# Copying the spread 1/sum out of PSUM on ScalarE, and multiplying on GpSimd

## The chip, the cores and the metric

The kernel runs on one core of a Trainium2 chip. A core has five engines that work side by side: TensorE (PE, matrix products into PSUM), VectorE (DVE), ScalarE (ACT), GpSimd (POOL, which works on SBUF alone here) and SyncE (SP, which issues the transfers in this kernel). Each takes its instructions in the order in which they are written. The metric is the device time of one execution in microseconds. Times of before are the median of three executions; all durations below come from one further execution that was profiled.

## What is computed

Attention with rotary positions over 2 batches of 8 heads, 576 positions and 64 features a head; its output is turned into 1152 tokens of 512 features and goes through two feed-forward layers.

```python
q_rot, k_rot = (rotate(q), rotate(k))
scores = scale * np.matmul(q_rot, k_rot.transpose(0, 1, 3, 2))
scores = scores - np.max(scores, axis=-1, keepdims=True)
attn = np.exp(scores)
attn = attn / (np.sum(attn, axis=-1, keepdims=True) + 1e-09)
x = np.matmul(attn, v)            # then (B, S, H * D) -> 1152 x 512
h = np.maximum(x @ w_in, 0.0)
x = h * h @ w_out                 # 512 -> 2048 -> 512
out = (x @ w_a) * (x @ w_b) @ w2_out   # 512 -> 1536 -> 512
```

## The kernel before

**Stages.** The sixteen heads are worked in eight pairs, p = 0 to 7. A pair's 576 query rows of two heads are 1152 rows, in nine tiles of 128: chunks c = 0 to 3 have one tile of each head, chunk 4, the tail, has 64 rows of each head in one tile. After the attention come the feed-forward layers, from about 136 us on (units of the first product are mixed in with the end of the attention) to the end, all on TensorE in products that are each split into three (high and low parts of both factors).

**A chunk.** TensorE writes scores of a chunk into PSUM tiles `s` (two slots of two banks each, so one chunk fills both). VectorE finds the row's minimum of the negated scores while it moves them to SBUF (L427), which frees the slot; ScalarE takes the exponential in place and sums it (L432, into `st`); VectorE transposes the result in blocks of 32 (L448, into `PT_wb` or `PT_acc`). In the same loop step TensorE multiplies V with the transposed exponentials of the pair before (`times_v`, L480, into four banks `av`).

**The sums.** The division comes after the product with V. `recip` inverts the 1152 sums of a pair on VectorE (L509, L510) and cuts them into three bf16 pieces on GpSimd (`part`, L513 to L516). `flip` turns the pieces on TensorE (L525) into a PSUM tile `r`, and ScalarE copies them to SBUF (`rows`, L309). `spread` has nine small products of TensorE (L539) write 1/sum over all partitions of that same tile `r`, which takes one of the two score slots at the tail of each pair from 2 on: at the tail of pair p it flips pair p - 1 and spreads pair p - 2. VectorE multiplies the attention's output `xf` with it straight out of PSUM (L546, two instructions of 128x288), and with that the slot is free. Then `x` is made: ScalarE rounds `xf` to the high part (L572), GpSimd subtracts (L569) for the low part. Pairs 6 and 7 are spread after the last scores, into the free columns 192 to 480 of two `av` banks; the flip of pair 7 uses a corner of `AV[2]`.

**Loads.** SyncE's queue carries everything that comes from HBM: `X` (queries, keys and their swapped halves, four loads of 288 KB a pair, into two buffers `g0` and `g1`), `V` (four loads of 288 KB a pair, each behind a tiny copy of ScalarE, L458, that says that the place is free) and the raw weights (512 KB each, three buffers). GpSimd multiplies and adds `X` into the rotated queries and keys (`rotate`, L358 and L359).

**What sets the order.** The program builds a list of operations with costs, dependencies and buffers (`Plan`), and a greedy planner assigns engines and an order from them; the instructions of TensorE, ScalarE, VectorE and GpSimd are kept in that order. SyncE is not in that list: its transfers were put in order by the framework's own scheduler.

Of the kernel before, what the change touches and what calls it, by code (L numbers as in the profile page):

```python
# [7 lines left out]
F32 = mybir.dt.float32  # L8
# [8 lines left out]
P = 128  # L17
# [22 lines left out]
VAT = ((0,), (1,), (2, 3), (), ())  # L40
WARM = (16, 2, 5, 3)
# [203 lines left out]
def attention_moe_moe2_kernel(ctx: ExitStack, tc: tile.TileContext, qk, rope, vq, ident_in, sel_in, w_in, w_out, w_a, w_b, w2_out, out):  # L245
# [39 lines left out]
    def narrow():  # L285
# [10 lines left out]
        "raw": 3, "bits": 2, "sums": 1, "cl": 2, "wa": NWA, **{f"P{k}": 1 for k in range(NPR)}, "v": NV, "u": 2,  # L296
# [157 lines left out]
    def load_part(p, c):  # L454
        ex, st = EXP[p, c][1], ST[p]
        for a in VAT[c]:
            r = slice(32 * a, 32 * a + 32)
            w = pl.op("ACT", ("us", 0.2), lambda e, r=r: e.copy(V4[r, p % 2, 0, 0, 0:1], st()[r, 1, 2 * c + 1:2 * c + 2]), ex[-1:] + ([AVD[p - 2]] if p > 1 else []))  # L458
            w.soon, w.anchor = 1.8, SDONE[p, c]
            LV.setdefault(p, []).append(dma(288, lambda e, r=r: e.dma_start(out=V4[r, p % 2], in_=vq[p]), [w]))  # L460
        if c < 4 and p + 2 < NPAIR:
            if c == 0:
                load_qk_done[p + 2] = load_qk(p + 2)
            before = EXP[order[5 * p + c - 1]][1] if p + c else []
            load_qk_done[p + 2][PLANES[c]] = LX[p + 2, c](before)
# [65 lines left out]
    def spread(p, slots, at):  # L531
# [11 lines left out]
        ends = []  # L543
        for r in range(2):
            q = slice(r * 288, r * 288 + 288)
            m = pl.op("DVE", ("p", 288), lambda e, r=r, q=q: e.tensor_tensor(out=xf()[:, q].rearrange("p (b n) -> p b n", b=2), in0=at[r](), in1=xf()[:, q].rearrange("p (b n) -> p b n", b=2), op=ALU.mult), [o] + XOK[p])  # L546
            m.soon, m.anchor = 0.9, o
# [3 lines left out]
            ends.append(m)  # L551
# [400 lines left out]
    def last_spread(p, slots=None):  # L952
        pair = [lambda r=r: AV[r]()[:, 192:480].rearrange("p (b n) -> p b n", b=2) for r in range(2)]
        b = [Buf("av", None)] if slots is None else slots
        ends = spread(p, b, pair)
        if slots is None:
            pl.op(None, None, None, ends, rel=b)
# [14 lines left out]
    for n, (fn, *a) in enumerate(steps):  # L972
# [6 lines left out]
        if n == FILL[1]:  # L979
            flip(p, [], lambda: AV[2]().bitcast(BF16)[0:27, 896:1024])  # L980
# [25 lines left out]
    with tc.manual_schedule(engines={getattr(mybir.EngineType, e) for e in ("PE", "Activation", "DVE", "Pool")}):  # L1006
        pl.run({"PE": pe, "ACT": act, "DVE": dve, "POOL": pool, "SP": nc.sync})
# [65 lines left out]
```

## Time and profile before

| What | us |
|---|---|
| median of three runs (561.53 to 564.47) | 563.22 |
| the profiled execution | 563.06 |
| its span (first to last instruction) | 561.0 |
| TensorE busy in the span | 541.4 |
| VectorE busy | 433.1 |
| ScalarE busy | 277.7 |
| GpSimd busy | 302.4 |

The span is what the rows below are counted in; 2.1 us of the execution lie around it. A busy TensorE is not TensorE at its best: matrix products overlap, and the clock that it is granted differs. What matters is therefore read by stretch: in which one TensorE waits, and for whom. The page of the profile gives shares for the whole span; the views of the trace give single instructions with their start, their duration and, in brackets, how long the engine was idle before them and who released it.

### The profile page before, as it was taken

To read this page: it belongs to the slowest core of one execution; us is meant where nothing else is said; L and a number is where in the kernel's file an instruction comes from. 1 tells how busy PE (TensorE), PEld (TensorE's weight loads), DVE (VectorE), ACT (ScalarE), POOL (GpSimd) and SP (SyncE) were. 2 spreads that over 40 slices of the span, in tenths; PEclk is the share of its full clock that TensorE was granted. 3 is DMA by queue.
4 is the path that set the end of the run, shared out by engine and by line. 5 is a ranking of instruction groups with operands and counts; after the bars stand their busy time and mean duration, and the time that the engine had idled before them with its cause. 6 is when DMAs were issued, how large, how long until landed. Compare 5 with 4: busy or idle time off the path is not lost.

```text
span 561.0 us, 13032 instructions
## 1 busy us (share of the span) xinstructions
PE 541.4 (96%) x5318; PEld 486.5 (87%) x5318; DVE 433.1 (77%) x785; ACT 277.7 (49%) x652; POOL 302.4 (54%) x249
## 2 busy tenths in 40 slices
PE   7898998999999999999999999999999999999997
PEld 6565665657899999999999999999999999999986
DVE  5998798998189589858865679987897888886454
ACT  2556675777367567416612445466544454434210
POOL 3956679722187347506622465785776666565000
PEclk9999898999899999999999999999999999999999
DMA  7677865333033444413420110124341222400004
GB/s 242 190 211 212 208 197 132 102 93 99 4 114 124 139 157 143 139 52 115 147 76 20 57 39 1 60 76 131 112 140 58 103 77 76 142 10 1 1 0 168
DMA packets 18911, 58.45 MB, mean 104 GB/s; under 512 B 2313, under 2 KB 4489, under 8 KB 17828
## 3 DMA queue, kind: packets, MB, share of 16 engines
q1 hardware_dynamic: 18852, 57.63, 32.9%
q8 instruction: 41, 0.67, 0.5%
q14 instruction: 18, 0.15, 0.1%
HBM read 55.26 MB, written 2.36 MB: 103 GB/s over the span
## 4 chain that ended last, share of the span: by engine, by line
PE 82%; DVE 12%; ACT 2%; issue 2%; DMA 1%; SPq 0%; POOL 0%; DVEq 0%; POOLq 0%
PE m L674 12%; PE m L676 12%; PE m L675 12%; PE av L480 7%; PE av L674 6%; PE av L676 6%; PE av L675 6%; PE s L407 6%; PE m L883 3%; PE m L882 3%; PE m L881 3%; DVE y L569 2%; DVE PT_acc L448 2%; DVE PV L427 2%; PE av L883 1%
## 5 line engine op out<-in xcount | busy, mean ns | idle before, releaser
L569 POOL TENSOR_TENSOR g<-v,g 128x384 fp32r<-128x384 f32 (+1 forms) x39 | 47.5, 1219 | 48.7 <-ACT g L572 48.4
L432 ACT ACTIVATE PV<-PV,st 128x576 f32<-128x576 f32 x48 | 36.9, 770 | 39.0 <-DVE PV L427 37.1
L572 ACT CAST g<-v 128x384 fp32r<-128x384 f32 (+1 forms) x72 | 40.8, 568 | 30.4 <-DVE v L852 16.2
L675 PE MATMUL m<-y,w_p 128*128 128x288 f32 x152 | 44.8, 295 | 0.0
L674 PE MATMUL m<-y,w_p 128*128 128x288 f32 x152 | 44.7, 294 | 0.0
L676 PE MATMUL m<-y,w_p 128*128 128x288 f32 x152 | 44.7, 294 | 0.0
L427 DVE TENSOR_SCALAR_CACHE_REDUCE PV<-s 128x576 f32<-128x576 f32 x48 | 34.3, 750 | 6.5 <-PE s L407 6.2
L358 POOL TENSOR_TENSOR X<-X,cs_rot 128x1152 f32<-128x1152 f32 x14 | 36.8, 2635 | 0.1
L407 PE MATMUL s<-cs_rot 64*128 64x288 f32 x128 | 27.1, 435 | 6.0 <-DVE PV L427 2.8
L480 PE MATMUL av<-PT_acc,PV 32*64 32x128 f32 (+1 forms) x1152 | 28.3, 312 | 4.2 <-issue 3.0
L480 PEld LDWEIGHTS av<-PT_acc,PV 32*64 32x64 f32 x1152 | 22.2, 139 | 10.1 <-issue 7.2
L713 DVE TENSOR_TENSOR v<-m,v 128x384 f32<-128x384 f32 x32 | 17.7, 552 | 16.5 <-ACT v L712 16.5
L407 PE MATMUL s<-rot 64*128 64x288 f32 x128 | 27.5, 461 | 2.8 <-DVE PV L427 1.5
L722 DVE TENSOR_TENSOR oacc<-m,oacc 128x512 f32<-128x512 f32 (+1 forms) x32 | 21.6, 679 | 10.8 <-PE m L883 10.7
L675 PEld LDWEIGHTS m<-y,w_p 128*128 128x128 f32 x152 | 28.5, 188 | 1.0
L676 PE MATMUL m<-g,w_o 128*128 128x384 f32 (+1 forms) x92 | 29.3, 319 | 0.0
L675 PE MATMUL m<-g,w_o 128*128 128x384 f32 (+1 forms) x92 | 29.3, 318 | 0.0
L674 PE MATMUL m<-g,w_o 128*128 128x384 f32 (+1 forms) x92 | 29.3, 318 | 0.0
L674 PEld LDWEIGHTS m<-y,w_p 128*128 128x128 f32 x152 | 28.5, 188 | 0.9
L569 POOL TENSOR_TENSOR w_i<-bits_i,w_i 128x512 fp32r<-128x512 f32 x10 | 13.1, 1306 | 29.1 <-ACT w_i L572 29.0
L569 DVE TENSOR_TENSOR g<-v,g 128x384 fp32r<-128x384 f32 (+1 forms) x33 | 24.2, 732 | 5.8 <-ACT g L572 5.6
L676 PEld LDWEIGHTS m<-y,w_p 128*128 128x128 f32 x152 | 28.6, 188 | 0.0
(246 smaller groups left out, 1919.3 us busy)
## 6 DMA issues: line engine op xcount, KB each, us to landing
PV<-in_vq SPq DMA_DIRECT2D x32, 288.0 KB, 4.2
raw_i<-in_w_in SPq DMA_DIRECT2D x16, 512.0 KB, 3.7
raw_o<-in_w_out SPq DMA_DIRECT2D x16, 512.0 KB, 3.6
X<-in_qk SPq DMA_DIRECT2D x26, 288.0 KB, 4.2
raw_a<-in_w_a SPq DMA_DIRECT2D x12, 512.0 KB, 3.7
raw_b<-in_w_b SPq DMA_DIRECT2D x12, 512.0 KB, 3.6
raw<-in_w_out SPq DMA_DIRECT2D x12, 512.0 KB, 3.7
out<-oacc SPq DMA_DIRECT2D x8, 256.0 KB, 2.0
```

Of the source, the lines that this page charges most:

```text
L358: m = pl.op(where, ("s", 2 * S), lambda e, qi=qi: e.tensor_tensor(out=x()[:, :, qi, :], in0=x()[:, :, qi, :], in1=cs, op=ALU.mult), [done[ ...
L407: pe.matmul(s[h]()[:, bk, 0:288], q0, k0[h][:, bk * 288:bk * 288 + 288], start=True, stop=True)
L427: m = pl.op("DVE", ("us", 0.7), lambda e, h=h, j=j: e.tensor_scalar(out=PP[pr.k][:, h, :].rearrange("p (b n) -> p b n", b=2), in0=s[h]()[: ...
L432: x = pl.op("ACT", ("us", 0.8), lambda e, h=h, j=j: e.activation(PP[pr.k][:, h, :], PP[pr.k][:, h, :], AF.Exp, bias=st()[:, 0, j:j + 1], s ...
L480: pe.matmul(AV[a]()[half(h), q], v[r, h, b], pt[r, k:k + 4 + both, 32 * b:32 * b + 32], start=(b == 0), stop=(b == KB - 1), skip_group_che ...
L569: e.tensor_tensor(out=out_, in0=a, in1=b, op=ALU.subtract)
L572: h = pl.op("ACT", ("s", n), lambda e: e.copy(hi_(), val()), after)
L674: pe.matmul(dst, wh, mh, start=first, stop=False, skip_group_check=open_)
L675: pe.matmul(dst, wh, ml, start=False, stop=False, skip_group_check=open_)
L676: pe.matmul(dst, wl, mh, start=False, stop=last, skip_group_check=open_)
L722: return pl.op("DVE", ("p", width), lambda e: e.tensor_tensor(out=acc(), in0=dst(), in1=acc(), op=ALU.add), [o] + b.prior, rel=[b])
L883: pe.matmul(b(), gt[:, 1, c], w[:, 0, d], start=False, stop=(k == H - 1))
```

## The change

ScalarE copies the spread 1/sum out of PSUM into an SBUF tile `inv` (one buffer, two copies of 128x288 a pair). The multiplication with `xf` reads `inv` and goes to GpSimd for pairs 0 to 5, and to GpSimd or VectorE, as the planner finds, for pairs 6 and 7. SyncE joins the engines that keep the planner's order. The four loads of `X` for pair p + 2 are given places in that order: chunk 0, chunk 1 and, two of them, chunk 3 of pair p, behind the chunk's tiny copy or exponential; a lateness of 1.5 us is reckoned for loads of `X` and `V`. The last spreads go to columns 0 to 288 of their banks, and the flip of pair 7 gets a bank of its own.

```diff
+XAT = ((0,), (1,), (), (2, 3), ())
+FAR = 1.5
...
-        "raw": 3, "bits": 2, "sums": 1, "cl": 2, "wa": NWA, **{f"P{k}": 1 for k in range(NPR)}, "v": NV, "u": 2,
+        "raw": 3, "bits": 2, "sums": 1, "cl": 2, "wa": NWA, **{f"P{k}": 1 for k in range(NPR)}, "v": NV, "u": 2, "inv": 1,
...
         ex, st = EXP[p, c][1], ST[p]
+        more = p + 2 < NPAIR
+        if c == 0 and more:
+            load_qk_done[p + 2] = load_qk(p + 2)
+        w = ex[-1]
         for a in VAT[c]:
...
-            LV.setdefault(p, []).append(dma(288, lambda e, r=r: e.dma_start(out=V4[r, p % 2], in_=vq[p]), [w]))
-        if c < 4 and p + 2 < NPAIR:
-            if c == 0:
-                load_qk_done[p + 2] = load_qk(p + 2)
-            before = EXP[order[5 * p + c - 1]][1] if p + c else []
-            load_qk_done[p + 2][PLANES[c]] = LX[p + 2, c](before)
+            d = dma(288, lambda e, r=r: e.dma_start(out=V4[r, p % 2], in_=vq[p]), [w])
+            d.late = FAR
+            LV.setdefault(p, []).append(d)
+        for k in XAT[c] if more else ():
+            d = load_qk_done[p + 2][PLANES[k]] = LX[p + 2, k]([w])
+            d.late = FAR
...
-        ends = []
+        inv = Buf("inv", lambda: sb.tile([P, S], F32, tag="inv", name=f"inv{p}"))
+        ends = [pl.op("ACT", ("p", 288), lambda e, r=r: e.copy(inv()[:, r * 288:r * 288 + 288].rearrange("p (b n) -> p b n", b=2), at[r]()), [o], acq=[] if r else [inv]) for r in range(2)]
+        turned = []
         for r in range(2):
             q = slice(r * 288, r * 288 + 288)
-            m = pl.op("DVE", ("p", 288), lambda e, r=r, q=q: e.tensor_tensor(out=xf()[:, q].rearrange("p (b n) -> p b n", b=2), in0=at[r](), in1=xf()[:, q].rearrange("p (b n) -> p b n", b=2), op=ALU.mult), [o] + XOK[p])
-            m.soon, m.anchor = 0.9, o
+            ends[r].soon, ends[r].anchor = 0.9, o
+            m = pl.op("POOL" if p < NPAIR - 2 else FLEX, ("s", 288), lambda e, q=q: e.tensor_tensor(out=xf()[:, q], in0=inv()[:, q], in1=xf()[:, q], op=ALU.mult), [ends[r]] + XOK[p])
+            turned.append(m)
...
-            ends.append(m)
+        pl.op(None, None, None, turned, rel=[inv])
...
-        pair = [lambda r=r: AV[r]()[:, 192:480].rearrange("p (b n) -> p b n", b=2) for r in range(2)]
+        pair = [lambda r=r: AV[r]()[:, 0:288].rearrange("p (b n) -> p b n", b=2) for r in range(2)]
...
-            flip(p, [], lambda: AV[2]().bitcast(BF16)[0:27, 896:1024])
+            b = bank("flip", 64)
+            pl.op(None, None, None, [flip(p, [b], lambda: b().bitcast(BF16)[0:27])], rel=[b])
...
-    with tc.manual_schedule(engines={getattr(mybir.EngineType, e) for e in ("PE", "Activation", "DVE", "Pool")}):
+    with tc.manual_schedule(engines={getattr(mybir.EngineType, e) for e in ("PE", "Activation", "DVE", "Pool", "SP")}):
```

SyncE's queue in pairs 2 and 3, before (X4 is the pair 4 of queries and keys, in_vq is V, in_w_in raw weights):

```order
L332 DMA X4_431<-in_qk 128x576 x4
L332 DMA X5_676<-in_qk 128x576 x4
L583 DMA raw_i0_475<-in_w_in 128x512
L460 DMA PV_73<-in_vq 32x2304 x4
L332 DMA X6_936<-in_qk 128x576 x4
L460 DMA PV_73<-in_vq 32x2304
```

The same place after:

```order
L592 DMA raw_i0_477<-in_w_in 128x512
L466 DMA PV_73<-in_vq 32x2304
L334 DMA X4_525<-in_qk 128x576
L466 DMA PV_73<-in_vq 32x2304
L334 DMA X4_525<-in_qk 128x576
L466 DMA PV_73<-in_vq 32x2304 x2
L334 DMA X4_525<-in_qk 128x576 x2
L592 DMA raw_i1_728<-in_w_in 128x512
L466 DMA PV_73<-in_vq 32x2304
L334 DMA X5_781<-in_qk 128x576
```

The four loads of a pair's X no longer stand together; they stand between the loads of V, and those of X5 to X7 stand about one pair later.

VectorE at the tail of pair 5, before (s5_4 holds the tail's scores, s6_0 the next pair's first; r5 the spread):

```order
L427 TENSOR_SCALAR rot_69,st5_1244<-s5_4_0_1422 128x576
L448 STREAM_TRANSPOSE PT_acc_72<-small_70 128x576
L546 TENSOR_TENSOR xf3_1253<-r5_1430,xf3_1253 128x288 x2
L448 STREAM_TRANSPOSE PT_acc_72<-small_70 128x576
L448 STREAM_TRANSPOSE PT_acc_72<-rot_69 128x576
L427 TENSOR_SCALAR PV_73,st6_1508<-s6_0_1_1478 128x576
```

And after:

```order
L429 TENSOR_SCALAR rot_69,st5_1245<-s5_4_0_1427 128x576
L450 STREAM_TRANSPOSE PT_acc_72<-small_70 128x576 x2
L450 STREAM_TRANSPOSE PT_acc_72<-rot_69 128x576
L429 TENSOR_SCALAR PV_73,st6_1513<-s6_0_1_1484 128x576
L429 TENSOR_SCALAR PV_73,st6_1513<-s6_0_0_1482 128x576
```

The two multiplies are gone from VectorE. ScalarE at the same tail, before:

```order
L432 ACTIVATE small_70,st5_1244<-small_70,st5_1244 128x576 x2
L309 COPY rows4_1443<-r5_1430 27x128
L432 ACTIVATE rot_69,st5_1244<-rot_69,st5_1244 128x576
L572 CAST x_67<-xf3_1253 128x288 x2
L432 ACTIVATE PV_73,st6_1508<-PV_73,st6_1508 128x576
```

And after:

```order
L434 ACTIVATE small_70,st5_1245<-small_70,st5_1245 128x576 x2
L311 COPY rows4_1447<-r5_1435 27x128
L550 COPY inv3_1475<-r5_1435 128x288 x2
L434 ACTIVATE rot_69,st5_1245<-rot_69,st5_1245 128x576
L434 ACTIVATE PV_73,st6_1513<-PV_73,st6_1513 128x576
```

The two copies stand between the copy of the row and the tail's exponential; the rounding of `x` (L581 after) has moved to later places. TensorE's order in the attention is unchanged.

## Rows read from the trace of the kernel before

**Rows 1.** Busy us (x instructions) by stretch: PE, PEld, DVE, ACT, POOL, clock, DMA, GB/s.
```profile
40.00:145.00 105.00, 94.43 (x2212) 65.92 (x2195) 88.54 (x203) 69.75 (x220) 64.48 (x69) 0.95 0.53 145
145.00:561.00 416.00, 411.73 (x2696) 395.92 (x2695) 313.35 (x519) 190.44 (x386) 213.62 (x159) 1.00 0.25 84
```
**Rows 2.** TensorE's waits from 40 to 145 us: total us, times, longest.
```profile
PE av L480 <- issue: 4.1, 3, 2.3
PE s L407 <- DVE PV L427: 2.5, 4, 0.7
PE s L407 <- DVE bits_i L591: 2.4, 4, 0.6
```
**Rows 3.** The attention's end in order of time: start, duration, instruction, [idle before].
```profile
138.72 0.49 ACT L712 ACTIVATE v<-m 128x384 f32<-128x384 f32 x1 [1.09 <-POOL rest L514]
...
139.72 0.81 DVE L546 TENSOR_TENSOR xf<-av,xf 128x288 f32<-128x288 f32 x2
...
140.22 4.63 PE L480 MATMUL av<-PT_acc,PV 32*64 32x160 f32 x128 [1.20 <-DVE xf L546]
```
**Rows 4.** The tail of pair 5 in order of time, same columns.
```profile
103.13 0.26 ACT L309 COPY rows<-r 27x128 bf16<-27x128 bf16 x1 [0.65 <-PE r L539]
...
103.36 0.78 ACT L432 ACTIVATE rot<-rot,st 128x576 f32<-128x576 f32 x1
103.94 0.79 DVE L546 TENSOR_TENSOR xf<-r,xf 128x288 f32<-128x288 f32 x2
...
104.05 2.03 PE L407 MATMUL s<-cs_rot 64*128 64x288 f32 x8
...
105.33 0.73 DVE L448 STREAM_TRANSPOSE PT_acc<-rot 128x576 f32<-128x576 f32 x1
...
106.11 0.76 DVE L427 TENSOR_SCALAR_CACHE_REDUCE PV<-s 128x576 f32<-128x576 f32 x1
...
106.97 0.78 ACT L432 ACTIVATE PV<-PV,st 128x576 f32<-128x576 f32 x1 [1.78 <-POOL rot L359]
```
**Rows 5.** TensorE alone in order of time, 53 to 100 us.
```profile
54.61 0.49 PE L480 MATMUL av<-PT_acc,PV 32*64 32x160 f32 x5 [2.31 <-issue]
55.03 1.32 PE L407 MATMUL s<-rot 64*128 64x288 f32 x8
...
58.12 1.89 PE L407 MATMUL s<-rot 64*128 64x288 f32 x8
...
87.80 1.24 PE L407 MATMUL s<-rot 64*128 64x288 f32 x8
```
**Rows 6.** ScalarE's groups by shape: busy us, mean ns of one, idle before.
```profile
L827 ACT COPY v<-m 128x288 f32<-128x288 f32 x16 | 6.4, 400 | 41.6 <-PE m L676 41.6
```
**Rows 7.** GpSimd's groups by shape, same columns.
```profile
L358 POOL TENSOR_TENSOR X<-X,cs_rot 128x1152 f32<-128x1152 f32 x14 | 36.8, 2635 | 0.1
L569 POOL TENSOR_TENSOR x<-xf,x 128x288 fp32r<-128x288 f32 x14 | 11.0, 797 | 10.3 <-ACT x L572 10.3
```
**Rows 8.** GpSimd's fullest pair, columns as in rows 1.
```profile
84.10:101.40 17.30, 15.36 (x341) 10.36 (x342) 14.84 (x34) 11.37 (x36) 13.43 (x13) 0.90 0.45 116
```
**Rows 9.** SyncE's issues ahead of TensorE's first stop, in order of time.
```profile
42.96 1.75 SPq L332 DMA_DIRECT2D X<-in_qk  x4
...
45.30 3.70 SPq L460 DMA_DIRECT2D PV<-in_vq  x4
```
**Rows 10.** From stop to stop of TensorE, columns as in rows 1.
```profile
54.60:67.59 12.99, 11.92 (x254) 8.35 (x253) 10.07 (x25) 8.69 (x28) 7.69 (x10) 0.87 0.77 204
67.59:86.79 19.20, 17.13 (x380) 11.37 (x381) 16.34 (x39) 12.61 (x40) 15.33 (x14) 1.00 0.69 191
```
**Rows 11.** The page's DMA queue for instructions: packets, MB, share of 16 engines.
```profile
q8 instruction: 41, 0.67, 0.5%
```
**Rows 12.** After the first stop, columns as in rows 1.
```profile
56.00:59.50 3.50, 3.50 (x58) 2.50 (x56) 2.54 (x8) 2.13 (x12) 1.97 (x6) 0.51 0.40 117
```
**Rows 13.** The granted clock in 40 slices of the span, in tenths, from the page.
```profile
PEclk9999898999899999999999999999999999999999
```

## The prediction

> **What bounds the kernel now.** I read the busy time by stretch first, then TensorE's waits, then the instructions in order of time at the places where those waits lie. A pair is two heads; chunks c = 0 to 4 are its score tiles, chunk 4 its tail. From 145 us to the end TensorE is busy for 411.73 of 416 us [rows 1]: an engine that is full there gives nothing back to helpers, and time can be won there only by arriving earlier. From 40 to 145 us it is busy for 94.43 of 105 us, at a mean granted clock of 0.95. So what the change can win lies in those 105 us: 10.6 us of idleness and what the slow clock costs. The waits that the trace names are few [rows 2]: 4.1 us in three waits that nothing in the profile releases ("issue"), 2.5 us on VectorE's L427 and 2.4 us on its L591. A further 1.20 us stands at 140.22 us behind the multiply L546 [rows 3]. Before 40 us VectorE and ScalarE alternate with no multiply among them, and I leave that stretch alone.
>
> **The tail of a pair, the change's first place.** The tail of pair 5 is the pattern for pairs 3, 5 and 6 (at pair 4 a stop of TensorE lies in its place, below). The tile r5 holds the spread 1/sum and takes one of the two score slots. VectorE frees it with two L546, from 103.94 to 104.73 us [rows 4]; until then the second half of pair 6's first scores can't start, so those eight records last 2.03 us, against 1.32 us where nothing is in the way [rows 5]: a wait of 0.7 us. VectorE then transposes the tail (to 106.06) and reduces the new scores at 106.11.
> Now ScalarE copies r5 out. Its copy of the row of 1/sum ends at 103.39; two copies of 128x288 out of PSUM at 400 ns [rows 6] end at 104.19, so the slot is free 0.54 us earlier. But they stand ahead of the tail's exponential, which starts at 104.2 instead of 103.36 and ends at 104.97; with 0.1 us for the hand-over, the transpose that needs it runs from about 105.1 to 105.8 (0.73 us). VectorE, rid of 0.79 us of multiplies, waits for it, and reduces at 105.8 instead of 106.11. So of 0.79 us taken off VectorE and 0.54 us off the slot, 0.3 us is left per tail: the exponential is what is late next. Three tails: 0.9 us. The bounds are 2.1 us (the whole 0.7 us three times) and a loss of 0.6 us (each of the four instructions in that row 0.12 us longer than taken).
>
> **GpSimd's new work.** It gets two multiplies a pair of the shape of its L569, 797 ns each [rows 7], so 1.6 us. Its fullest pair, 84.1 to 101.4 us, has 13.43 us of work in 17.3 us [rows 8]; 15.0 us still fits. I cost it at nothing, the cover being 2.3 us a pair. If it runs out, ScalarE pays: the rounding of x (L581) now waits in ScalarE's queue for GpSimd, with exponentials behind it, and ScalarE's copy into the single buffer inv waits for the multiplies of the pair before.
>
> **The end of attention.** TensorE is idle until 140.22, since the last pair's output needs the banks that hold the spread for pair 6, and VectorE reads them from 139.72 on, behind its product L713, which waits for ScalarE's ReLU (138.72 to 139.21) [rows 3]. ScalarE's copies come right behind that ReLU: 139.61 and 140.01 in place of 140.1 and 140.53. That is 0.5 us; bounds 0 and 1.2 us. The flip in its own bank and the spread at columns 0 to 288 keep TensorE's order, and the eight copies that must precede that spread are done a unit earlier: nothing, and at most 0.2 us.
>
> **SyncE's queue.** This is the larger term, and the less certain. Before, the four loads of X5 go out together at 42.96 us, then w_in, then four loads of V from 45.30 [rows 9]: 8 x 288 + 512 = 2816 KB in 6 us. In that wake TensorE stops for 2.31 us at 52.30, in the midst of one matmul group whose operands it had already used [rows 5]. The stops are regular: from the first to the second TensorE runs 254 + 253 = 507 instructions, to the third 380 + 381 = 761 [rows 10], two and three times 253.6. Queue q8 brings instructions, 41 packets with 0.67 MB, so 16 KB in each [rows 11]. So I read a stop as a block of instructions that arrives late, and the data ahead of it as the reason.
> After, X loads go out one or two a chunk, between the loads of V, and X5 moves from pair 2 to pair 3. In the 6 us ahead of the first stop this leaves X4 and V of pair 2, with at most four loads (1152 KB) together: under half the backlog. I take the first stop as gone, and 2.0 of its 2.31 us as won, 0.3 us going back to a slot wait that it now hides. The other two, 1.8 us together, I leave as they are: 512 KB loads of weights stay near them, and X6 and X7 move into pairs 4 and 5. The bounds of all stops together are a gain of 4.1 us and a loss of 4.1 us (as many again in the two pairs that now load X).
> What else is moved: V of pair 0 now goes ahead of X2, and each X load waits behind V's gate on ScalarE. X5's last loads then leave near 66 us (the chunk 3 of pair 3) instead of 44; its rotation, four instructions of at most 2.64 us each [rows 7], is wanted at 87.80 [rows 5]: nothing, with some 10 us of cover.
>
> [...]
>
> **The sum** is 0.9 + 0.5 + 2.0 + 1.2 = 4.6 us. The profiled execution took 563.06 us (span 561.0 and 2.1 around it), 0.2 us under the median of 563.22; 563.06 - 4.6 = 558.5 us.
>
> **The rivals.**
> First, the stops stay. If a block of instructions doesn't wait for the data ahead of it, its lateness comes from elsewhere and the order of loads is nothing to it. Then the tails and the end alone count: 563.06 - 1.4 = 561.7 us. For it: TensorE's instruction stream is the same, so the same blocks are fetched at the same points. Against it: all three stops lie in pairs 2 to 4, the last that load X (X5, X6 and X7 stand in that order in SyncE's queue); pairs 5 to 7, with V and weights alone, have none. [...] No row shows the turn-taking; chance 0.25.
> Second, slower: GpSimd comes late and ScalarE's queue carries it. If a multiply waits at each tail for one L358 (2.64 us, [rows 7]), it ends at 104.2 + 2.64 + 0.8 = 107.6, the rounding of x behind it near 108.1, while the next pair's first exponential is due at 106.7 (106.97 before, [rows 4], less the 0.3): 1.4 us late at each of six tails, 8.4 us, less the 4.6: 563.06 + 3.8 = 566.9. It decides from 0.8 us a tail. For it: the new order puts the multiply behind an L358 in most pairs. Against it: only at some tails does the rounding stand directly ahead of the next exponential. Chance 0.1.
> [...] Chance 0.1.
>
> **How the numbers follow.** The forecast has 0.55, the rivals 0.25, 0.1 and 0.1. The range from 554.0 to 562.5 us takes in all but the slower one and the far ends of the stops' bounds. A change within 0.5% (2.8 us) is about what a measurement of this kernel can't tell from none. Faster by more means under 560.4: the forecast less some 0.05 for a sum that falls short, and the third rival, 0.6; within 0.5%: 0.29; slower: 0.11, the second rival and a share for new stops in pairs 4 and 5.
>
> **What would show it.** Right: no "issue" wait over 2 us near 52 us and no slow stretch behind it; the first scores of pairs 4, 6 and 7 in 1.5 us instead of 2.03; VectorE idle before the transpose of the tail's last tile; TensorE's wait at the end near 0.7 us. Wrong: the same three stops at the same blocks; ScalarE waiting for GpSimd ahead of L581 or of the copies into inv; TensorE waiting in the weights' stage after 150 us, whose order of VectorE and GpSimd has moved too.

## The result, and the profile after

The changed kernel took 556.5 us (median of four executions, 554.64 to 559.76), before 562.94 us beside it: a ratio of 0.988, 95% interval 0.984 to 0.992, so 1.2% faster and clear of noise. In a later series it took 557.89 against 565.38 (0.986, 0.983 to 0.990). The ratios leave out single executions over 1.5% slower than the fastest of their kernel, in which the granted clock was low too (0.979 to 0.985). The forecast was 558.5 us within 554.0 to 562.5, faster. The time came out as forecast; how it comes about did not in all parts, as what follows shows.

The profiled execution took 554.64 us with a span of 552.9, 8.1 us under that of before. The stages first (columns as in [rows 1]):

```profile
40.00:137.00 97.00, 89.55 (x2175) 62.43 (x2173) 88.00 (x189) 72.89 (x234) 75.35 (x82) 0.98 0.58 161
137.00:552.90 415.90, 411.73 (x2695) 395.73 (x2693) 313.44 (x521) 190.58 (x388) 213.15 (x158) 1.00 0.24 84
```

The second row is the weights' stage: TensorE has the same 411.73 us of work as in [rows 1] and the same 416 us for it. All of the gain was made ahead of it: VectorE's last tail reduction starts 5.7 us earlier (128.18 instead of 133.91), and from there to the end it takes 424.7 us instead of 427.1. TensorE's waits from 40 to 140 us (total, times, longest), to be set against [rows 2]:

```profile
PE s L409 <- DVE PV L429: 4.1, 5, 1.1
PE s L409 <- DVE bits_i L600: 2.4, 4, 0.6
PE av L486 <- ACT inv L550: 0.5, 1, 0.5
PE s L409 <- issue: 0.3, 1, 0.3
```

Of the three stops ("issue", 4.1 us) none is left; a wait of 0.3 us stands at another place. The wait on VectorE's reduction (L427, now L429) has grown from 2.5 to 4.1 us: something new stands there. The tail of pair 5 in order of time, against [rows 4]:

```profile
97.94 0.76 DVE L429 TENSOR_SCALAR_CACHE_REDUCE rot<-s 128x576 f32<-128x576 f32 x1 [0.38 <-PE s L404]
...
98.51 0.26 ACT L311 COPY rows<-r 27x128 bf16<-27x128 bf16 x1 [0.35 <-PE r L545]
98.62 0.08 DVE L429 DVE_READ_ACCUMULATOR rot<-s 128x1 f32 x1
98.62 1.44 DVE L450 STREAM_TRANSPOSE PT_acc<-small 128x576 f32<-128x576 f32 x2
98.67 0.68 ACT L550 COPY inv<-r 128x288 f32<-128x288 f32 x2
99.25 0.77 ACT L434 ACTIVATE rot<-rot,st 128x576 f32<-128x576 f32 x1
99.43 1.24 PE L409 MATMUL s<-cs_rot 64*128 64x288 f32 x8
...
100.15 0.78 DVE L450 STREAM_TRANSPOSE PT_acc<-rot 128x576 f32<-128x576 f32 x1
...
100.85 0.72 DVE L429 TENSOR_SCALAR_CACHE_REDUCE PV<-s 128x576 f32<-128x576 f32 x1
```

VectorE goes from one transpose to the next without a wait: the two of `small` end at 100.06, that of the tail's own tile starts at 100.15. The exponential that it needs ends at 100.02, just in time. The two copies took 0.68 us together, where the forecast took 2 x 0.40. TensorE's eight records last 1.24 us instead of 2.03. I measure a tail from the start of VectorE's reduction of the last tile to the start of its next reduction: here 100.85 - 97.94 = 2.91 us. Before it is 3.55, 106.11 of [rows 4] less the start of this line of before:

```profile
102.56 0.76 DVE L427 TENSOR_SCALAR_CACHE_REDUCE rot<-s 128x576 f32<-128x576 f32 x1 [0.37 <-PE s L402]
```

The tail of pair 6 is the one in which the exponential is late after all (3.14 us); there a conversion of weights stands ahead of the copies in ScalarE's queue:

```profile
115.38 0.78 DVE L450 STREAM_TRANSPOSE PT_wb<-rot 128x576 f32<-128x576 f32 x1 [0.32 <-ACT rot L434]
```

At the end of the attention the wait of 1.20 us [rows 3] is 0.51 us:

```profile
133.34 0.70 ACT L550 COPY inv<-av 128x288 f32<-128x288 f32 x2
...
133.79 2.72 PE L486 MATMUL av<-PT_acc,PV 32*64 32x160 f32 x128 [0.51 <-ACT inv L550]
```

And the new thing, in pair 4 (GpSimd, VectorE and TensorE, put together from the three engines' own lists):

```profile
70.51 2.63 POOL L360 TENSOR_TENSOR X<-X,cs_rot 128x1152 f32<-128x1152 f32 x1
```
```profile
70.98 2.19 DVE L515 TENSOR_SCALAR st<-st 128x9 f32<-128x9 f32 x1
...
73.35 0.75 DVE L429 TENSOR_SCALAR_CACHE_REDUCE PV<-s 128x576 f32<-128x576 f32 x1
```
```profile
74.16 1.91 PE L409 MATMUL s<-cs_rot 64*128 64x288 f32 x8 [1.15 <-DVE PV L429]
```

An instruction on nine columns, 0.13 us at its shortest, takes 2.19 us: I call this a collision. It ends at 73.17, 0.03 us after GpSimd's rotation (70.51 + 2.63 = 73.14). The next reduction is late by that, and TensorE waits 1.15 us. In pair 5 the same again: 2.30 us, ended at 89.87, the rotation at 89.85. What holds the instruction, no row shows.

The clock row of the page has one 8 left after the start, where [rows 13] has three:

```profile
PEclk9999998999999999999999999999999999999999
```

**The account of the two profiles.** A pair's period runs from the reduction of one tail to that of the next. A half-clock stretch is one in which the granted clock is about half of its 1.00 elsewhere: before it was 0.51 from 56.0 to 59.5 us [rows 12], 0.52 from 93.5 to 97.0 and 0.50 from 141.4 to 144.8, after 0.50 from 87.3 to 90.7; beside the collision of pair 4, from 70.5 to 73.2 us, it was 1.00. From the tail of pair 2 on, which starts at 50.80 us before and at 50.73 after:

| period of pair | before | after | what lies in it |
|---|---|---|---|
| 3 | 18.73 | 13.97 | before: two stops (2.31, 1.07) and a half-clock stretch; after: a shorter tail |
| 4 | 15.77 | 16.60 | after: shorter tail, one collision |
| 5 | 17.26 | 16.63 | before: a stop of 0.69 and a half-clock stretch; after: a collision and a half-clock stretch |
| 6 | 15.68 | 15.00 | the shorter tail, nothing else |
| 7 | 15.68 | 15.23 | the shorter tail |

Together -5.7 us. The end adds 0.7 (1.20 to 0.51) and the half-clock stretch behind the wait of 1.20 us, in which the 128 records of [rows 3] took 4.63 us; they take 2.72 now, 1.9 us less. That makes 8.3 us, and the spans differ by 8.1.

### The profile page after: what moved, and what is told of

Same layout as the page of the kernel before. It is cut to its first block, busy times and chain, and to the rows that moved or that the text cites. A ratio compares the mean times of both kernels' runs of the same rounds, so it can differ in the third digit from the quotient of the medians.

```text
span 552.9 us, 13053 instructions
## 1 busy us (share of the span) xinstructions
PE 537.3 (97%) x5318; PEld 483.4 (87%) x5318; DVE 432.8 (78%) x774; ACT 280.9 (51%) x668; POOL 312.0 (56%) x260
## 4 chain that ended last, share of the span: by engine, by line
PE 81%; DVE 10%; ACT 4%; DMA 2%; issue 1%; SPq 1%; DVEq 0%; ACTq 0%
PE m L683 13%; PE m L685 13%; PE m L684 13%; PE av L683 7%; PE av L685 6%; PE av L684 6%; PE av L486 4%; PE s L409 4%; PE m L892 3%; PE m L891 3%; PE m L890 3%; DVE PV L429 2%; DVE PT_wb L450 2%; DMA X<-in_qk 2%; PE av L892 1%; PE av L891 1%
## 5 line engine op out<-in xcount | busy, mean ns | idle before, releaser
L578 POOL TENSOR_TENSOR g<-v,g 128x384 fp32r<-128x384 f32 (+1 forms) x37 | 45.5, 1232 | 37.1 <-ACT g L581 36.9
L581 ACT CAST g<-v 128x384 fp32r<-128x384 f32 (+1 forms) x72 | 40.6, 567 | 28.9 <-DVE v L861 16.2
L684 PE MATMUL m<-y,w_p 128*128 128x288 f32 x144 | 42.4, 295 | 0.0
L683 PE MATMUL m<-y,w_p 128*128 128x288 f32 x144 | 42.3, 294 | 0.0
L685 PE MATMUL m<-y,w_p 128*128 128x288 f32 x144 | 42.3, 294 | 0.0
L429 DVE TENSOR_SCALAR_CACHE_REDUCE PV<-s 128x576 f32<-128x576 f32 x48 | 34.0, 744 | 1.2 <-PE s L409 1.2
L603 POOL TENSOR_SCALAR cl_i<-cl_i 128x512 f32<-128x512 f32 x12 | 23.3, 1944 | 11.6 <-DVE v L722 5.8
L683 PE MATMUL m<-x,w_i 128*128 128x384 f32 x88 | 29.8, 339 | 0.0
L685 PE MATMUL m<-x,w_i 128*128 128x384 f32 x88 | 29.4, 334 | 0.0
L684 PE MATMUL m<-x,w_i 128*128 128x384 f32 x88 | 29.4, 334 | 0.0
L684 PEld LDWEIGHTS m<-y,w_p 128*128 128x128 f32 x144 | 27.0, 188 | 1.0
L683 PEld LDWEIGHTS m<-y,w_p 128*128 128x128 f32 x144 | 27.0, 188 | 0.8
```

The lines of the kernel that those rows point to most:

```text
L429: m = pl.op("DVE", ("us", 0.7), lambda e, h=h, j=j: e.tensor_scalar(out=PP[pr.k][:, h, :].rearrange("p (b n) -> p b n", b=2), in0=s[h]()[: ...
L578: e.tensor_tensor(out=out_, in0=a, in1=b, op=ALU.subtract)
L581: h = pl.op("ACT", ("s", n), lambda e: e.copy(hi_(), val()), after)
L603: e.tensor_scalar(out=dst(), in0=cl(), scalar1=-HI * TURN, scalar2=HI, op0=ALU.max, op1=ALU.min)
L683: pe.matmul(dst, wh, mh, start=first, stop=False, skip_group_check=open_)
L684: pe.matmul(dst, wh, ml, start=False, stop=False, skip_group_check=open_)
```

## The experiments

Two tables gather what many profiles show of two terms, the tails and the stops; the runs follow one by one. The tails are those of pairs 2 to 6, read as above (pair 7's has no reduction behind it), in us:

| who empties the slot | kernel | tails of pairs 2 to 6 |
|---|---|---|
| VectorE, by multiplying out of PSUM | loads alone, with and without the addition | 3.64, 3.65, 3.55, 3.55, 3.55: together 17.94 |
| ScalarE, by copies; GpSimd multiplies | the changed kernel, both times | 2.91, 2.91, 2.91, 2.91, 3.14: together 14.78 |
| ScalarE, by copies; VectorE multiplies out of SBUF | one | 3.72, 3.91, 3.91, 3.92, 3.07 |

The kernel before has 3.55 in its last two, too; stops lie in others of its tails.

| loads of X | TensorE's "issue" waits from 40 to 145 us, one profile each |
|---|---|
| as before | 4.1, 5.0, 5.2, 2.1 |
| four together, in the planner's order | 2.4, 1.6 |
| spread, as in the change | 0.3, 0.4, 0.4, 0.4, 0.2, 1.6, 2.6 |

The kernel with the exponential first, spread as well, has 0.3 us of them and beside these four waits of 0.80 us, also named "issue", where the others wait for VectorE to free a score slot. The two last rows are set apart from the first by most of their numbers, not by all: 2.1 stands among the old loads and 2.6 among the new.

**SyncE's part alone.** Before, with the loads of the change and SyncE in the list, and nothing else:

```diff
+XAT = ((0,), (1,), (), (2, 3), ())
...
+        for k in XAT[c] if more else ():
+            d = load_qk_done[p + 2][PLANES[k]] = LX[p + 2, k]([w])
...
-    with tc.manual_schedule(engines={getattr(mybir.EngineType, e) for e in ("PE", "Activation", "DVE", "Pool")}):
+    with tc.manual_schedule(engines={getattr(mybir.EngineType, e) for e in ("PE", "Activation", "DVE", "Pool", "SP")}):
```

> The kernel before with SyncE's part of the change alone: SyncE joins the planner's order and the loads of X are spread over chunks 0, 1 and 3; VectorE still multiplies out of PSUM. Forecast's theory (a backlog of loads holds back blocks of TensorE's instructions): the stop of 2.31 us near 52 us is gone, and with it the half-clock stretch behind it; by the forecast's terms 2.0 + 1.2 = 3.2 us less than before, about 559.8 us; if all three stops go as in the changed kernel, 4.1 us and one or two slow stretches (1.2 us each) less, 556.5 to 558. Rival (the loads are nothing to the stops; the moved work of ScalarE, VectorE and GpSimd shifted them): three waits named issue, 4.1 us together, stay, and the time is within 0.5% of before, 560 to 565 us.

Measured: 562.66 us, ratio 0.998 (0.995 to 1.001). The stops are gone, and the time is the same. TensorE's waits:

```profile
PE s L409 <- DVE PV L429: 2.9, 5, 0.7
PE s L409 <- DVE bits_i L597: 2.4, 4, 0.6
PE av L486 <- DVE xf L552: 1.2, 1, 1.2
PE s L409 <- issue: 0.2, 1, 0.2
PE av L486 <- issue: 0.2, 1, 0.2
```

The period of pair 3 is 14.54 instead of 18.73, so 4.2 us were won there. Pair 5, where before had a stop and a half-clock stretch, takes 16.19 instead of 17.26. But pair 4 takes 18.36 instead of 15.77, pair 6 16.54 and pair 7 16.93 instead of 15.68. In pair 4 stands, beside a half-clock stretch from 72.4 to 79.2 us (the mean granted clock of this profile is 0.988):

```profile
71.21 2.63 POOL L360 TENSOR_TENSOR X<-X,cs_rot 128x1152 f32<-128x1152 f32 x1
```
```profile
72.06 1.81 DVE L515 TENSOR_SCALAR st<-st 128x9 f32<-128x9 f32 x1
```

The rotation ends at 73.84, VectorE's instruction at 73.87. There is no multiply on GpSimd in this kernel: the collision belongs to the loads. X comes about a pair later, and the planner then puts the rotation ahead of the pieces of the sums in GpSimd's queue, beside VectorE's inversion, where before it stood behind them. In pair 5 the instruction takes 1.19 us, in pair 6 1.53 us; pair 7's loss is a half-clock stretch.

**The rest alone.** The change without SyncE's part:

```diff
-XAT = ((0,), (1,), (), (2, 3), ())
...
-    with tc.manual_schedule(engines={getattr(mybir.EngineType, e) for e in ("PE", "Activation", "DVE", "Pool", "SP")}):
+    with tc.manual_schedule(engines={getattr(mybir.EngineType, e) for e in ("PE", "Activation", "DVE", "Pool")}):
```

> The changed kernel without SyncE's part: the copies on ScalarE, the multiply on GpSimd and the banks of the end as changed, but SyncE's queue and the loads of X as in the kernel before. Forecast's theory: the three stops stay (4.1 us of waits named issue), the tails give 0.9 us (0.3 each; up to 0.64 each by the profile of the changed kernel, 1.9) and the end 0.5: 560.6 to 561.7 us. Rival 1 (this part carries the whole gain, and the stops go with it): 556 to 558 us, no issue wait over 0.5 us. Rival 2 (the multiplies on GpSimd put a long rotation beside VectorE's sum operation of 128x9, which then takes over 2 us instead of 0.17): one or two such instructions at 1 to 2 us each eat the gain, 562 to 565 us.

Measured: 558.11 us, the median of five executions between 555.77 and 561.18 (559.12 with a sixth at 564.52); ratio 0.989 (0.979 to 0.999). The stops are all there:

```profile
PE av L480 <- issue: 4.7, 3, 2.9
PE s L407 <- DVE PV L427: 2.8, 4, 0.7
PE s L407 <- DVE bits_i L594: 2.4, 4, 0.6
PE av L480 <- ACT inv L544: 0.5, 1, 0.5
PE s L407 <- issue: 0.3, 1, 0.3
```

Tails without a stop in them are 2.91 us, the end waits 0.5, and between the first sum instruction (0.97 us) and the last, at the end of the attention (0.63 us), none takes over 0.24 us. So this part carries most of the gain with every stop in place: 5.4 us by the medians (563.56 to 558.11), with a wide interval, where the forecast gave it 1.4 and the best case written ahead of this run 2.4.

**The loads together again.** The changed kernel with

```diff
-XAT = ((0,), (1,), (), (2, 3), ())
+XAT = ((0, 1, 2, 3), (), (), (), ())
```

> The changed kernel with one thing put back: the four loads of a pair's X go out together, in chunk 0 of pair p, still in the planner's order. Theory of the backlog: eight loads of 288 KB stand together again, and TensorE stops with nothing to release it (issue) at one to three of its blocks, 1 to 4 us together; 557.5 to 561 us. Rival (the stops came from the order that the framework gave to SyncE's queue, such as X5 ahead of V, not from four loads together): no issue wait over 0.5 us and the time of the changed kernel, 555.5 to 557.5 us.

Measured: 555.61 us, ratio 0.988 (0.982 to 0.994). Issue waits of 2.4 us came back, as the backlog theory says; the time did not follow. Between the first sum instruction (1.11 us) and the last, at the end of the attention (0.64 us, as in the changed kernel), the longest is 0.50 us here: with early loads the rotations of 2.63 us miss VectorE's inversion. By these profiles stops were exchanged for collisions.

**The places of the stops.** Before, with the warming products at the start changed so that everything later moves by 128 instructions of TensorE:

```diff
-            for k in range(n):
+            z = ZERO.bitcast(BF16)
+            for k in range(8 if after is zeros else n):
                 pe.matmul(b()[:, 0:P], ZERO, ZERO, start=True, stop=True)
+            for k in range(80 if after is zeros else 0):
+                pe.matmul(b()[0:32, 0:2], z[:, 0:32], z[:, 0:2], start=True, stop=True)
```

> The kernel before with 8 of the 16 warming products at the start replaced by 80 tiny ones (two columns), which shifts everything that TensorE does afterwards by 128 instructions; nothing else. In the kernel before the three long stops come at TensorE's instruction numbers 1461, 1968 and 2729, which are 181, 176 and 169 modulo 256. Theory (a stop is a block of instructions that arrives late, and blocks have a fixed length): the stops move in the program; counted from the new start they lie at 165 to 185 modulo 256 again, so at other products than before (128 instructions earlier or later). Rival (the stop belongs to the product, or to a moment in the queue of transfers, and the regular spacing is chance): the same products stop, now at 37 to 57 modulo 256.

Measured: one execution, 567.96 us, span 566.2, issue waits of 5.2 us. The stretches from the start to the stops, first of before (the second and third stop), then of this kernel; in brackets TensorE's products and weight loads so far:

```profile
0.00:66.30 66.30, 59.08 (x984) 41.27 (x984) 53.65 (x119) 35.05 (x104) 40.79 (x38) 0.97 0.75 215
0.00:85.85 85.85, 76.18 (x1364) 52.55 (x1365) 70.34 (x156) 48.02 (x143) 56.29 (x52) 0.98 0.74 210
```
```profile
0.00:63.20 63.20, 58.55 (x984) 40.50 (x984) 52.65 (x113) 32.33 (x98) 40.69 (x38) 1.00 0.73 210
0.00:82.50 82.50, 75.10 (x1364) 51.69 (x1365) 69.88 (x151) 45.97 (x139) 54.08 (x50) 1.00 0.75 209
```
```profile
64.63 0.53 PE L483 MATMUL av<-PT_wb,PV 32*64 32x160 f32 x15 [1.18 <-issue]
...
84.88 1.59 PE L483 MATMUL av<-PT_acc,PV 32*64 32x128 f32 x37 [2.10 <-issue]
```

The stops come after exactly the same number of instructions, 984 + 984 = 1968 and 1364 + 1365 = 2729, though other products stand there. (The one at 1461 is missing; one at 858 + 858 = 1716 has come, 255 further on.) In these two profiles a stop belongs to a place in the instruction stream, not to a product: so much of the theory stands. That a block of instructions arrives late there, no row shows. The other profiles agree. Apart from the four slot waits named above, every issue wait of TensorE's in the fourteen profiles comes after 948, 1204, 1461, 1716, 1968, 2220 to 2224, 2470, 2726 to 2729, 3230, 3995 or 5515 to 5527 products and weight loads: steps of about 250 to 257, or whole multiples of that.

**The addition left out.** In the changed kernel, in before with SyncE's part, and in before. The sums are at least 1, so that adding 1e-9 changes no float32 number; these kernels leave the addition out:

```diff
         def inverse(e):
-            e.tensor_scalar_add(st()[:, 1, :], st()[:, 1, :], 1e-9)
             e.reciprocal(st()[:, 1, :], st()[:, 1, :])
```

In the changed kernel:

> The changed kernel without the addition of 1e-9 to the sums (a row's sum is at least 1, so the float32 sum is the same number without it). In the changed kernel that 128x9 instruction of VectorE takes 2.19 and 2.30 us in pairs 4 and 5, both times while GpSimd runs a 128x1152 rotation, and 0.13 to 0.24 us elsewhere. Theory (VectorE is held for as long as GpSimd's instruction runs, and TensorE's wait of 1.15 us behind the first comes from it): no VectorE instruction of that line over 0.3 us, the wait gone, 0.8 to 2 us less than the changed kernel, 554.5 to 555.7 us. Rival (the reciprocal that follows is held in its place, or the time is hidden in the slow clock there): RECIPROCAL of 2 us, or the same 556 to 557 us.

Measured: 553.64 us, ratio 0.985 (0.979 to 0.991). Pairs 4 and 5 take 15.02 and 15.11 us instead of 16.60 and 16.63, and the reciprocals 0.21 us at most; that of pair 4 ran inside a rotation (70.25 to 72.88 us) in 0.17 us and was not held. By pair 4 a collision costs 1.6 us where the clock is full. Pair 5 lost a half-clock stretch with its collision, and the two don't add up: together they cost 1.6 us, a half-clock stretch alone costs 1.25 (below). (The notes ahead of this run and of the control leave out the last addition, at the end of the attention: 0.64 us in the changed kernel, 0.52 in before.) But the changed kernel's time was from another series, so both were run side by side:

> The changed kernel itself, once more, so that the next three are set beside it on the same chip. Expected 556 to 557.5 us; how often VectorE's 128x9 instruction takes over 1 us, and in which pairs the clock is halved, may differ from the first profile: with two such collisions again the periods of pairs 4 and 5 are 16.6 us, otherwise 15.0.

> The changed kernel without the addition of 1e-9 to the sums, beside the changed kernel on the same chip. Theory (VectorE held by GpSimd's rotation in pairs 4 and 5 costs 1.6 us a pair in the changed kernel): 2 to 3.2 us less than the changed kernel, 553 to 554.5 us, pairs of 15.0 us where the clock is full. Rival (the 2.9 us between the first runs of the two came from a different chip or clock): less than 1 us apart.

Measured: 557.89 us with the addition (0.986, 0.983 to 0.990), 557.09 without (0.985, 0.982 to 0.989). The difference is 0.8 us, inside both intervals: the rival's number. The changed kernel has its collision in pair 4 again (2.19 us, period 16.60), and one of 1.47 us in pair 6, which beside a half-clock stretch (0.50 from 105.5 to 108.7 us) takes 16.25 us, as long as a pair with such a stretch alone. But the other kernel lost as much elsewhere in its profile, with a half-clock stretch in pair 4 (mean granted clock of the profile 0.994) and, in spite of the spread loads, a stop in pair 5 (two loads of V and two of X had gone out together just ahead, from 79.25 us on):

```profile
PE av L486 <- issue: 2.3, 2, 2.2
PE s L409 <- DVE PV L429: 2.1, 3, 0.8
```

So the price of a collision at the full clock is shown, and that leaving the addition out makes the changed kernel faster is not.

In before with SyncE's part, and in before itself:

> The kernel before with SyncE's part of the change alone, and without the addition of 1e-9 to the sums (which changes no float32 number, since a sum is at least 1). With SyncE's part alone the stops were gone (0.4 us of issue waits instead of 4.1) and the time the same, 562.66 us; VectorE's 128x9 sum instruction took 1.81, 1.19 and 1.53 us there in pairs 4 to 6. Theory (the loads that come later push GpSimd's rotations onto that instruction, which gives the stops' gain back): without it 3 to 5 us less than with SyncE's part alone, 557.5 to 559.5 us. Rival (the gain went to something else, such as half-clock stretches): 561.5 to 563.5 us.

> The kernel before without the addition of 1e-9 to the sums (no float32 number changes). The control for the two kernels in which that addition is left out: in the profile of before the instruction took 0.13 to 0.40 us, never over. Theory (only a collision with GpSimd's rotation makes it dear): at most its own time, eight times 0.2, so 562 to 565 us, the same within 0.3%. Rival (the instruction is dear in itself, and its absence gives the same 3 us here as in the changed kernel): 560 to 561 us.

Measured: 561.19 us, ratio 0.994 (0.991 to 0.997), and 563.06 us, 0.997 (0.994 to 1.001). With the loads the absence of the addition is worth 1.5 us between the medians (562.66 to 561.19), against 3 to 5 expected. The control gained 1.2 us between its own medians (564.29 to 563.07), at a ratio that can't be told from none. So that collisions took the gain of SyncE's part isn't shown by the times. The clock of each execution tells more. At a mean granted clock of 0.996 and over, three executions with the addition took 560.2 to 562.2 us and three without it 556.6 to 558.3; at 0.988 and under, six took 562.0 to 563.0 and four 561.4 to 562.7. By their clock the three fast ones without it had no half-clock stretch and the three with it one, which is about 1.3 us of the 3.6 between them. That leaves some 2 us for the collisions where the clock is full; beside several stretches the difference is 0.6. These are few executions, but they are in line with the periods above.

> The changed kernel without the addition of 1e-9 and with the four loads of a pair's X together in chunk 0 again. With the addition, the four loads together had brought issue waits of 2.4 us back and yet the time of the changed kernel, since the rotations then no longer met the 128x9 instruction. Theory (spreading the loads takes the stops away and pays with collisions; without collisions the stops stand alone): issue waits of 1.5 to 4 us, and 1.5 to 3 us more than the kernel without the addition whose loads are spread, 555 to 556.5 us. Rival (the stops cost nothing where VectorE sets the pace): the same within 0.8 us, 553 to 554.3 us.

Measured, with `XAT` as in the run with the loads together: 558.14 us (0.987, 0.982 to 0.991), issue waits of 1.6 us. Against 557.09 us with spread loads it is 1.1 us slower, inside the intervals. That the spreading helps where there are no collisions is not shown.

**The multiply on VectorE.** The changed kernel with

```diff
-            m = pl.op("POOL" if p < NPAIR - 2 else FLEX, ("s", 288), lambda e, q=q: e.tensor_tensor(out=xf()[:, q], in0=inv()[:, q], in1=xf()[:, q], op=ALU.mult), [ends[r]] + XOK[p])
+            m = pl.op("DVE" if p < NPAIR - 2 else FLEX, ("s", 288), lambda e, q=q: e.tensor_tensor(out=xf()[:, q], in0=inv()[:, q], in1=xf()[:, q], op=ALU.mult), [ends[r]] + XOK[p])
```

> The changed kernel with the multiply of pairs 0 to 5 back on VectorE, now out of inv in SBUF; the copies stay on ScalarE. Theory of the tail (two things were won: the slot is free earlier, by the copies, and VectorE is rid of 0.8 us per pair): the slot's part stays, VectorE's part is lost where VectorE sets the pace, 0.6 us at each of six tails, and more if a multiply meets a rotation on GpSimd: 558 to 562 us. Rival (the copies alone bring it, the multiply is placed where VectorE has time): 556 to 557 us like the changed kernel.

Measured: 560.9 us, ratio 0.994 (0.991 to 0.997). The slot is emptied by the copies as in the change, yet the tail is 3.91 us. In the tail of pair 5:

```profile
102.13 2.65 POOL L360 TENSOR_TENSOR X<-X,cs_rot 128x1152 f32<-128x1152 f32 x1
```
```profile
103.82 1.26 DVE L555 TENSOR_TENSOR xf<-inv,xf 128x288 f32<-128x288 f32 x1
...
105.00 0.77 DVE L450 STREAM_TRANSPOSE PT_acc<-rot 128x576 f32<-128x576 f32 x1
```

One multiply takes 1.26 us out of SBUF beside the rotation, two took 0.79 us out of PSUM before [rows 4], with a rotation beside them too (102.90 to 105.54 us). The other multiply of each pair, away from the tail and from a rotation, takes 0.40 to 0.45 us. At the tail of pair 6 no rotation runs (GpSimd is idle from 119.5 to 122.1 us):

```profile
121.14 0.42 DVE L555 TENSOR_TENSOR xf<-inv,xf 128x288 f32<-128x288 f32 x1
121.47 0.77 DVE L450 STREAM_TRANSPOSE PT_wb<-rot 128x576 f32<-128x576 f32 x1
122.16 0.72 DVE L429 TENSOR_SCALAR_CACHE_REDUCE PV<-s 128x576 f32<-128x576 f32 x1
```

There the tail is 3.07 us, against 3.55 before and 2.91 without a multiply. So in the one tail without a collision 0.5 of the 0.64 us stays, though VectorE multiplies: with the result copied out, one of the two multiplies can wait for a better place. In the other tails the collision takes that back and more. On GpSimd the multiply has no part in it.

**The exponential first.** The changed kernel, with the tail's exponential made due ahead of the copies:

```diff
+            if tail and p > 1:
+                x.soon, x.anchor = 0.5, o
             ex.append(x)
```

> The changed kernel with the exponential of a pair's last tile ahead of the two copies of the spread 1/sum in ScalarE's queue (pairs 2 to 7). The forecast held that behind the copies the exponential is what is late next at a tail. By that the tail (from VectorE's reduction of the last tile to its next one, 2.91 us in the changed kernel, 3.55 to 3.64 before) gets 0.1 to 0.3 us shorter, six times: 0.6 to 1.8 us less, 554.7 to 556 us. Rival (VectorE goes through its three transposes without a gap, and the exponential is in time): the tail stays at 2.8 to 2.95 us, the slot comes free 0.8 us later without anyone waiting for it, and the time is the same, 556 to 557.5 us.

Measured: 558.24 us (0.986, 0.981 to 0.991), as the changed kernel beside it. It doesn't decide the point: the planner answered by moving two instructions of the weights' conversion into VectorE's tail, ahead of the transpose, and the measure of the tail (5.3 us and more) holds them. TensorE waited 0.80 us for the slot there, four times. What the changed kernel's own trace says stands above: VectorE doesn't wait for the exponential in the tails of pairs 2 to 5, and waits 0.32 us in that of pair 6.

## Why the prediction came out right, and which of its steps did not

**Where the gain lies: right; the end was too small.** Nothing was won behind 137 us, and the wait at the end fell by 0.7 us (forecast 0.5). What the sum left out is the half-clock stretch behind that wait, the last of the three 8s of [rows 13], of which the sum takes one. In the nine profiles with the copies it is gone (2.72 to 2.84 us for the 128 records); four of the five with VectorE's multiply have it (4.53 to 4.75), and the fifth, the loads alone without the addition, shows the wait without the stretch:

```profile
136.61 2.99 PE L486 MATMUL av<-PT_acc,PV 32*64 32x160 f32 x128 [1.20 <-DVE xf L551]
```

From the last tail reduction to the end of the span those four take 427.1 or 427.2 us, the fifth 425.6, the nine 424.7 to 425.4: 1.7 to 2.5 us in place of 0.5. What keeps the clock up there isn't shown.

**The tails: mechanism right, the term too small by 2.3 us.** I had 3 x 0.3 = 0.9 us. The traces give 17.94 - 14.78 = 3.2 us for five tails, 0.63 each. Two steps failed. The copies take 0.68 us together, not 0.80, and the exponential begins before the second has quite ended, so that "the exponential is late next" misses by the 0.3 us on which it rested: it starts 1.31 us after the reduction, not 1.64, and is in time by 0.04 us. Only where it is late, in the tail of pair 6, does the tail come near the 3.24 us that I reckoned (3.14). And I counted three tails, leaving out two under which a stop or a slow clock lay, as though such a tail had nothing to give: those of pairs 2 and 4 went from 3.64 and 3.55 to 2.91 like the others.

**SyncE's queue: the loads bear on the stops, but were worth less.** I took the first stop as gone and left the others. All three went in this profile, and the shift by 128 instructions shows that they belong to places in the instruction stream (1968 and 2729 instructions from the start in both kernels). That a block of instructions arrives late there was my reading; no run shows it. That the order of the loads bears on them is shown by the kernels with the old and the new loads: 2.1 to 5.2 us against 0.2 to 2.6. It doesn't rule them out: a stop of 2.18 us came with spread loads too. The first rival (the stops stay) is out; of the turn-taking that stands beside its chance no run shows anything. But the sum gave this part 3.2 of 4.6 us, and alone it brought 0.17%, some 1 us, with an interval that holds nothing at all. The step that failed is "X5's last loads leave near 66 us instead of 44: nothing, with some 10 us of cover". I asked only whether the rotation is there when TensorE wants it, and not what it meets on the way: VectorE's inversion, for 1.6 us where that falls on the path at the full clock.

**The clock: price right, count not foreseeable.** A half-clock stretch in an otherwise undisturbed pair makes it 16.25 us instead of 15.00: 1.25 us. No run shows the 1.2 us that the sum has for the stretch behind the first stop; these 1.25 us, of another stretch, are what the runs show in their place. The 16.25 are pair 6 of the changed kernel without the addition, in its first run, with a granted clock of 0.50 from 101.5 to 104.7 us:

```profile
99.02 0.72 PE L409 MATMUL s<-cs_rot 64*128 64x288 f32 x2 [0.72 <-DVE PV L429]
100.35 1.22 PE L409 MATMUL s<-cs_rot 64*128 64x288 f32 x6 [0.61 <-DVE bits_i L599]
101.49 2.44 PE L486 MATMUL av<-PT_acc,PV 32*64 32x160 f32 x64
```

The 64 records of L486 take 2.44 us there, and 1.36 at 92.02 us of the same profile. Just ahead TensorE had waited twice, at the boundary of two pairs; the same two waits (0.72 and 0.60 us) stand ahead of the stretch of the changed kernel's first profile, and the stop of 2.31 us ahead of the first one of before. But the same two waits stand at the three other boundaries of that profile without the addition as well, with the full clock behind them (the mean granted clock of that profile, 0.997, has room for one stretch), so what decides stays open. Over 49 executions of before the mean granted clock was 0.988, over 10 of the changed kernel 0.993; a stretch is 0.003 of it (3.4 us at 0.50, in 560), so nearly four such stretches became a little over two. The sum had three become two. A straight line through those 49 gives 1.4 us for a stretch, near the 1.25.

**GpSimd's multiplies: right.** ScalarE waited for one 2.6 us in two waits, and TensorE for none; the second rival, whose price was 8.4 us, is out.

So errors cancelled, and that the time came out so near is in part luck: the tails brought 2.3 us more than I gave them and the end up to 2 us more, the loads alone about 2 us less. By the two parts run alone the forecast's 1.4 and 3.2 us were 5.4 and 1. The third rival, with its chance of 0.1, came nearest: in it the other stops go too. But the profiled execution's 554.64 us came about by other terms, with two collisions in it. What stays open is how much of the loads' gain is lost to collisions and how much to half-clock stretches: the kernels without the addition differ from those with it by 0.8, 1.5 and 2.9 us, depending on the loads and the series.

## What to carry to other kernels

When the busiest helper engine is relieved of an instruction, count every repetition of the place, also those where another wait covers it in the profile at hand. When a load is moved, follow the work that it releases to the place where it will now run, and ask what runs beside it there, not only whether it is still in time. And don't add up the prices of two delays in the same pair before you have seen them together.

## What the runs showed of the hardware that I had not expected

- A nine-column VectorE instruction ended only after GpSimd's rotation of 2.63 us had: in three profiles seven such instructions took 1.19 to 2.30 us, where one takes 0.13 us alone, and each ended 0.02 to 0.04 us after the rotation. The rotation, which had begun first each time, kept its 2.63 us. It holds for all: in the nine profiles with the addition 31 of these instructions took over 0.3 us, and each had started inside an instruction of GpSimd's and ended 0.03 us after it; three of them stand in the kernel before (0.32 to 0.52 us). The reciprocal on the same nine columns was never held (0.17 to 0.22 us), also in the middle of a rotation.
- A multiply with both inputs in SBUF took 1.26 us beside a rotation and 0.40 to 0.45 away from one, while the two with one input in PSUM took 0.79 us together [rows 4], inside a rotation as well.
- TensorE's stops lie at the same places of the instruction stream, 1968 and 2729 instructions from the start in two kernels whose products there differ; whether a given place stops changes from run to run.
- Back to back, two 128x288 copies out of PSUM took 0.68 to 0.70 us on ScalarE, less than twice the 0.40 us that one takes alone [rows 6].
